# Folding w_in's last quarters as sums and differences of its halves, and reordering the row loads, in a fused FFT and expert kernel

**The chip, the cores and the metric.** One NeuronCore of one Trainium2 chip. The metric is the device time of one launch in microseconds (us), median of several executions. In the profile PE is TensorE's matmuls, PEld its weight loads, DVE VectorE, ACT ScalarE, POOL GpSimd, SP the engine that issues most of the transfers.

## The reference

```python
# x: 8 x 3008 x 256, w_in: 256 x 2048, w_out: 2048 x 256, all float32
X = np.fft.fft(np.fft.fft(x, axis=1), axis=2).real    # 2-D DFT, real part
h = X.reshape(24064, 256) @ w_in
g = h * np.cos(h)
out = g @ w_out
```

## The kernel before

The DFT over the 256 channels is never carried out on x: it is multiplied into w_in. Each quarter (512 columns) of w_in becomes cosine weights `Wc` and sine weights `Ws`; this is "a fold of a quarter". The symmetry of the DFT halves the channels: rows of x are added to and subtracted from their mirror images, which gives the E part (sums) and the O part (differences). Matmuls with the constants `MC` make from them the real and imaginary sequences `Rr` and `Ir`. Then come 376 equal steps of about 5 us. A step makes P = Wc·Rr, adds Q = Ws·Ir in the same bank, and takes h_plus = P + Q and h_minus = 2P - (P + Q); `E` is ACT's copy of 2P, so Q may only start when E is done. Sines, products g and the second matmuls X1 and X2 (with `w` and `WT`) follow. The events of the steps are sorted by a planned time; T = 4.8 us is the period of the plan, not of the chip.

The order of the first loads, and the fold of a quarter:

```python
    for j in ORDER:                       # (0, 3, 2, 1): the four row tensors of x
        load_x(0, j)                      # two plain loads each
    for g in gathers(0, ORDER):           # two indirect loads each
        gather_x(*g, table=None if g[1] else first_ix)
    CC = cpool.tile([128, 512], FP, tag="CC")
    ... # cut: definitions
    spin(out=CC, in_=CC_dr.ap())          # channel cosines and sines
    load_w1(0)
    load_mats(0)
    load_w1(1)
    ... # cut
    def fold_mms(q, part, tag):
        ps = bank(tag)
        for h in range(2):                # both halves of the 256 channels
            mm(ps, CC[:, h * 256 + part : h * 256 + part + 128], w1[q][:, h], h == 0, h == 1)
        return ps
    def fold_copy(q, ri):
        act((Ws if ri else Wc)[:, q * 512 : (q + 1) * 512], pending.pop((q, ri)))
    ... # cut
    def mm_Q(i):
        first_mm(i, Ws, Ir, 127)
```

The start of the program: dummy matmuls, then the first quarter, DVE's folds of x and the first DFTs:

```python
    def warm(n):
        w = bank("M")
        for _ in range(n):
            mm(w, ones[:, 0:128], ones[:, 128:640], True)
    warm(72)
    ... # cut
    fold_mm(0, 1)
    fold_mm(0, 0)
    ... # cut
    fold_now("e0 o0 e3 o3 e2 E2 S0 e1 R0")
    halve_now(0, VE[3])
    first_x = Dft(0, 0, 0, fold_first(), Rb, True)
    ... # cut: copies, the first matmuls of the DFTs
    fold_now("o2 O2 o1 O0 J0")
    add_O(2, 0)
    halve_now(1, VO[3])
```

In the row folds the two sources are channels 1 to 127 and their mirror images, `src[:, :, 1:128]` and `src[:, :, 255:128:-1]`, with steps 1 and -1.

## Time and profile before

| | kernel before |
|---|---|
| time, three runs | 1924.75 us (1924.59 to 1925.07) |
| the profiled run | 1924.51 us, span 1922.5 us |
| PE busy | 1905.5 us, 99% of the span |
| granted clock after 15 us | 1.00 in each stretch of 5 us |

PE is busy nearly all the time, so a change to the opening counts only by when PE enters its long row of steps. The prediction below shows PE's, DVE's and ACT's lines. Two lines of DVE's timeline (start, length, what it computes, and in brackets the idle time before), then two of the groups by shape on POOL (count, busy us, mean ns of one, idle before):

```profile
11.93 1.21 DVE L375 TENSOR_TENSOR e<-xl 96x1016 f32<-96x1016 f32 x1 [0.33 <-issue]
...
21.26 1.60 DVE L375 TENSOR_TENSOR e<-e 96x512 f32<-96x512 f32 x3
```

```profile
L375 POOL TENSOR_TENSOR o<-xl 96x635 f32<-96x635 f32 x19 | 28.4, 1493 | 0.0
L375 POOL TENSOR_TENSOR e<-xl 96x635 f32<-96x635 f32 x17 | 27.5, 1617 | 0.0
```

Before the fold of the second row tensor DVE stands for 0.33 us ("issue": the profile names no releaser), and the E part is finished at 21.26 + 1.60 = 22.86. POOL's row folds take 1.5 to 1.6 us for 635 columns.

### The profile page before, as it was taken

How to read it: one execution, taken by the hardware profiler on the slowest of the kernel's cores; microseconds unless marked ns; L12 is line 12 of the kernel's file. 1: busy time of each engine (PE TensorE's matmuls, PEld its weight loads, DVE VectorE, ACT ScalarE, POOL GpSimd, SP SyncE). 2: the span in 40 equal slices, each digit the busy share in tenths (PEclk: the TensorE clock that was granted, in tenths of full speed). 3: DMA queues.
4: the chain of work that ended last, by engine and by line, in shares of the span. 5: the costliest groups of instructions: out<-in, count | busy, mean ns of one | idle time of the engine just before them, and what ended most of it. 6: DMA issues, size and time to landing. Idle time of an engine off the chain costs nothing.

```text
span 1922.5 us, 28941 instructions
## 1 busy us (share of the span) xinstructions
PE 1905.5 (99%) x9011; PEld 1652.4 (86%) x9011; DVE 1451.9 (76%) x2364; ACT 1519.3 (79%) x2994; POOL 1522.4 (79%) x2045
## 2 busy tenths in 40 slices
PE   8999999999999999999999999999999999999998
PEld 4888888888888888888888888888888888888887
DVE  6898777777777777777777777777777777777777
ACT  4777788878878887888778887888878887877886
POOL 6789888988888888888889898888888676655564
PEclk9999999999999999999999999999999999999999
DMA  9524311322023122311222113311112110100101
GB/s 201 39 66 77 63 28 31 61 39 54 16 61 46 43 41 45 59 30 33 51 58 37 39 22 60 52 45 30 27 29 37 21 21 16 17 12 12 23 10 25
DMA packets 259969, 80.58 MB, mean 42 GB/s; under 512 B 240393, under 2 KB 243256, under 8 KB 259816
## 3 DMA queue, kind: packets, MB, share of 16 engines
q1 hardware_dynamic: 248456, 48.65, 15.1%
q0 software_dynamic: 9184, 29.83, 8.4%
q8 instruction: 72, 1.18, 0.3%
q14 instruction: 81, 0.66, 0.1%
q10 hardware_dynamic: 2176, 0.26, 0.1%
HBM read 36.72 MB, written 24.69 MB: 32 GB/s over the span
## 4 chain that ended last, share of the span: by engine, by line
PE 90%; ACT 4%; DVE 4%; issue 1%; POOL 0%; DVEq 0%; POOLq 0%
PE H L298 35%; PE pC L298 16%; PE pD L298 16%; PE pB L298 15%; PE pA L298 8%; ACT G L310 1%; PE M L298 1%; DVE G L840 1%; DVE G L304 1%; ACT E L310 1%; ACT z L310 1%; ACT M L310 1%; DVE v L304 1%; ACT H L310 0%; DVE M L304 0%
## 5 line engine op out<-in xcount | busy, mean ns | idle before, releaser
L307 POOL TENSOR_TENSOR G<-G 128x256 f32<-128x256 f32 x1500 | 1084.4, 734 | 351.4 <-DVE G L840 277.2
L840 DVE SCALAR_TENSOR_TENSOR G<-H,G 128x512 f32<-128x512 f32 x376 | 259.2, 689 | 219.0 <-ACT G L310 216.6
L304 DVE TENSOR_TENSOR G<-H,G 128x512 f32<-128x512 f32 x376 | 259.7, 691 | 214.5 <-ACT G L310 211.3
L298 PE MATMUL H<-Ir,Ws 127*128 127x256 f32 x1504 | 387.7, 379 | 4.0 <-ACT E L310 4.0
L298 PE MATMUL H<-Rr,Wc 128*128 128x256 f32 x1504 | 388.1, 380 | 0.9 <-ACT H L310 0.9
L298 PE MATMUL pC<-G,WT 128*128 128x256 f32 x1504 | 387.5, 380 | 0.7 <-DVE u L304 0.7
L310 ACT ACTIVATE H<-Rb,wex 128x256 f32<-128x256 f32 x752 | 359.9, 479 | 23.6 <-DVE G L840 9.8
L310 ACT ACTIVATE G<-H 128x512 int32<-128x512 f32 x376 | 223.8, 595 | 178.7 <-DVE G L304 177.8
L310 ACT ACTIVATE E<-H 128x512 f32<-128x512 f32 x376 | 223.8, 595 | 163.2 <-PE H L298 161.7
L298 PEld LDWEIGHTS H<-Ir,Ws 127*128 127x128 f32 x1504 | 283.5, 189 | 48.6 <-ACT E L310 8.5
L298 PEld LDWEIGHTS pC<-G,WT 128*128 128x128 f32 x1504 | 285.2, 190 | 42.7 <-PE H L298 1.5
L298 PEld LDWEIGHTS H<-Rr,Wc 128*128 128x128 f32 x1504 | 281.4, 190 | 40.8 <-ACT H L310 3.0
L310 ACT ACTIVATE G<-G,halfpi 128x512 f32<-128x512 f32 x376 | 269.3, 716 | 2.7 <-DVE G L304 1.8
L304 DVE TENSOR_TENSOR G<-E,H 128x512 f32<-128x512 f32 x376 | 255.5, 679 | 5.3 <-PE H L298 5.3
L304 DVE TENSOR_TENSOR M<-G,M 128x512 f32<-128x512 f32 x376 | 257.6, 685 | 0.0
L840 DVE SCALAR_TENSOR_TENSOR G<-G,M 128x512 f32<-128x512 f32 x376 | 254.4, 677 | 0.5 <-ACT M L310 0.5
L310 ACT ACTIVATE M<-M,halfpi 128x512 f32<-128x512 f32 x376 | 245.6, 653 | 0.0
L298 PE MATMUL pB<-G,WT 128*128 128x256 f32 x752 | 224.6, 380 | 0.2 <-POOL G L307 0.2
L298 PE MATMUL pA<-G,w 128*128 128x256 f32 x752 | 223.8, 379 | 0.0
L310 ACT ACTIVATE M<-G 128x512 int32<-128x512 f32 x376 | 223.7, 595 | 0.0
L298 PE MATMUL pB<-G,w 128*128 128x256 f32 x752 | 223.7, 379 | 0.0
L298 PE MATMUL pD<-G,WT 128*128 128x256 f32 x752 | 223.7, 379 | 0.0
(164 smaller groups left out, 2066.0 us busy)
## 6 DMA issues: line engine op xcount, KB each, us to landing
out_dram<-ot SPq DMA_DIRECT2D x496, 32.0 KB
xl<-in_x_dram SPq DMA_DIRECT2D x64, 192.0 KB
e<-e POOLq DMA_DIRECT2D x22, 384.0 KB, 4.9
o<-o POOLq DMA_DIRECT2D x22, 381.0 KB, 4.8
out_dram<-ot SPq DMA_DIRECT2D x256, 2.0 KB
Rb<-r SPq DMA_DIRECT2D x10, 376.0 KB
w<-in_moe_w_in_dram SPq DMA_DIRECT2D x4, 512.0 KB
out_dram<-ot SPq DMA_DIRECT2D x64, 28.0 KB
```

The source lines that it names most:

```text
L298: nc.tensor.matmul(out_, lhsT=lhsT, rhs=rhs, start=start, stop=stop, skip_group_check=True)
L304: pin(nc.vector.tensor_tensor(out=o, in0=a, in1=b, op=op))
L307: pin(nc.gpsimd.tensor_tensor(out=o, in0=a, in1=b, op=op))
L310: pin(nc.scalar.activation(out=o, in_=i, func=func, **kw))
L840: nc.vector.scalar_tensor_tensor(out=o, in0=h, scalar=TWO_PI, in1=c, op0=ALU.mult, op1=ALU.mult)
```

## The change

The intent is to take work off PE in the opening. With halves a and b of a quarter of w_in, an even output channel of the DFT needs only a + b and an odd one only a - b. Two of the four quarters are folded so: DVE makes the sums and differences, and PE needs one matmul per part in place of two. Even and odd outputs lie apart in `CC`, `Wc` and `Ws`, so the folds of x must give even and odd channels apart too: their sources now have steps 2 and -2. The row loads are put in the order in which they are wanted, and 8 + 1 dummies go.

```diff
-    for j in ORDER:
-        load_x(0, j)
-    for g in gathers(0, ORDER):
-        gather_x(*g, table=None if g[1] else first_ix)
+    CC = cpool.tile([128, 512], FP, tag="CC")
+    load_x(0, 0)
+    spin(out=CC, in_=CC_dr.ap())
+    for n, g in enumerate(gathers(0, ORDER)):
+        gather_x(*g, table=None if g[1] else first_ix)
+        if n == 1:
+            pin(nc.gpsimd.memset(L[3][0:1, 0:1], 0.0))
+    for j in ORDER[1:]:
+        load_x(0, j)
...  # cut
+    def fold_mm(q, part, tag="H"):
+        ps = pending[q, part] = bank(tag)
+        cc = CC.rearrange("p (h k d) -> p h k d", h=2, k=2)[:, :, part]
+        if q in diffs:
+            mm(ps, cc[:, 0], diffs[q] if part else w1[q][:, 0], True)
+            return
         for h in range(2):
+            mm(ps, cc[:, h], w1[q][:, h], h == 0, h == 1)
+    def half_sum(q, part):
+        a, b = w1[q][:, 0], w1[q][:, 1]
+        if part:
+            diffs[q] = (Rb if q % 2 else Rr)[:, RING - 512 :]
+            vtt(diffs[q], a, b, SUB)
+        else:
+            vtt(a, a, b, ADD)
...  # cut: two copies per part, each of 64 partitions
     def take_last(q):
+        copy = act if q > 1 else lambda o, i: pin(nc.gpsimd.tensor_copy(out=o, in_=i))
...  # cut
-            lo, hi = src[:, :, 1:128], src[:, :, 255:128:-1]
+            lo = src[:, :, 1:129].rearrange("p m (j r) -> p m r j", r=2)
+            hi = src[:, :, 255:127:-1].rearrange("p m (j r) -> p m r j", r=2)
...  # cut
-    warm(72)
+    warm(64)
...  # cut: the events of the first steps, moved; the halves summed:
+        (1.1, lambda: half_sum(2, 1)),
+        (1.1, lambda: half_sum(2, 0)),
-        (1.5, lambda: warm(3)),
+        (0.5, lambda: warm(2)),
-    dve_all(1, FOLD["Q1"])
+    for n, part in ((1, 1), (2, 0)):
+        on_dve(n, 0.62, lambda part=part: half_sum(3, part))
+    dve_all(2, FOLD["Q1"])
```

Both copies of one part of the second quarter (`fold_copy(1, 1)`) go to DVE, and the step-4 copies of quarters 1 and 2 (`take_last`) to POOL. Two smaller moves are not shown: the third and fourth quarters of w_in are loaded ahead of w_out, and the second step's E is planned at 0.3 in place of 0.9, ahead of the sines.

More of the change, by code (lines that the diff above doesn't have):

```diff
@@ L82, in _chan_consts @@
 def _chan_consts():
-    c = np.arange(256)
-    d = np.arange(129)
-    cos = np.cos(2.0 * np.pi * ((c[:, None] * d[None, :]) % 256) / 256) / TWO_PI
-    d = np.arange(1, 128)
-    sin = -np.sin(2.0 * np.pi * ((c[:, None] * d[None, :]) % 256) / 256) / TWO_PI
-    m = np.concatenate([cos[:, :128], sin, cos[:, 128:]], axis=1)
+    th = 2.0 * np.pi / 256
+    c = np.arange(256)[:, None]
+    even, odd = np.arange(0, 128, 2)[None], np.arange(1, 128, 2)[None]
+    m = np.concatenate(
+        [
+            -np.sin(th * (c * even[:, 1:] % 256)),
+            np.cos(th * (c * 128 % 256)),
+            np.cos(th * (c * even % 256)),
+            np.cos(th * (c * odd % 256)),
+            -np.sin(th * (c * odd % 256)),
+        ],
+        axis=1,
+    )
+    m /= TWO_PI
     return np.ascontiguousarray(
@@ L170 @@
     pin(nc.vector.memset(ones, 1.0))
-    pin(nc.gpsimd.memset(zero, 0.0))
     ix = cpool.tile([NP, 9], U32, tag="ix")
@@ L212, in load_first @@
         spin(out=L[1][0:1, 7 * ND :], in_=x[b : b + 1, 0, :])
-    for j in ORDER:
+    CC = cpool.tile([128, 512], FP, tag="CC")
[6 more added lines that the diff above has]
+    for j in ORDER[1:]:
         load_x(0, j)
-    for g in gathers(0, ORDER):
-        gather_x(*g, table=None if g[1] else first_ix)
-    CC = cpool.tile([128, 512], FP, tag="CC")
-    pin(nc.gpsimd.memset(CC[0:1, 0:1], 0.0))
+    pin(nc.gpsimd.memset(zero, 0.0))
     w1, MC = [], []
@@ L233, in load_w1 @@
         t = spool.tile([128, n], FP, tag=tag, bufs=bufs, name="w1")[:, 0:1024]
+        if not q:
+            pin(nc.gpsimd.memset(t[0:1, 0:1], 0.0))
         w1.append(t.rearrange("p (h c) -> p h c", h=2))
@@ L250, in load_w2 @@
         )
-    spin(out=CC, in_=CC_dr.ap())
     load_w1(0)
@@ L256 @@
     load_mats(1)
+    load_w1(2)
+    load_w1(3)
     load_w2(0, 4)
     load_w2(4, NF)
-    load_w1(2)
-    load_w1(3)
     load_mats(2)
@@ L273 @@
     Rr = cpool.tile([128, RING], FP, tag="Rr")
-    Ir = cpool.tile([127, RING], FP, tag="Ir")
+    Ir = cpool.tile([128, RING], FP, tag="Ir")
     Rb = cpool.tile([128, RING], FP, tag="Rb")
@@ L281 @@
     r4_dr = dpool.tile([1, NB], FP, tag="r4", name="r4")
-    WD = (128, 127)
-    E = [cpool.tile([128, NS * 128], FP, tag=f"e{j}", name=f"e{j}") for j in range(4)]
-    O = [cpool.tile([128, NS * 127 + 1], FP, tag=f"o{j}", name=f"o{j}") for j in range(4)]
-    Z = [cpool.tile([128, 4 * w + ri], FP, tag=f"z{ri}", name=f"z{ri}") for ri, w in enumerate(WD)]
-    for t in (O[1], O[2], O[3], Z[1]):
-        pin(nc.gpsimd.memset(t[0:NP, t.shape[1] - 1 :], 0.0))
+    WD = (129, 128)
+    E = [cpool.tile([128, NS * WD[0]], FP, tag=f"e{j}", name=f"e{j}") for j in range(4)]
+    O = [cpool.tile([128, NS * WD[1]], FP, tag=f"o{j}", name=f"o{j}") for j in range(4)]
+    Z = [cpool.tile([128, 4 * w], FP, tag=f"z{ri}", name=f"z{ri}") for ri, w in enumerate(WD)]
     def bank(tag):
@@ L292, in bank @@
         return ppool.tile([128, 512], FP, tag=tag, bufs=bufs, name=tag)
+    ADD, SUB = ALU.add, ALU.subtract
     ACC = ("pA", "pB", "pC", "pD")
@@ L310, in act, with fold_copy @@
         pin(nc.scalar.activation(out=o, in_=i, func=func, **kw))
-    def fold_mms(q, part, tag):
-        ps = bank(tag)
-        for h in range(2):
-            mm(
-                ps,
-                CC[:, h * 256 + part : h * 256 + part + 128],
-                w1[q][:, h],
-                h == 0,
-                h == 1,
-            )
-        return ps
-    pending = {}
-    def fold_mm(q, ri, tag="H"):
-        pending[q, ri] = fold_mms(q, 128 * ri, tag)
-    def fold_copy(q, ri):
-        act((Ws if ri else Wc)[:, q * 512 : (q + 1) * 512], pending.pop((q, ri)))
+    pending, diffs = {}, {}
+    def fold_mm(q, part, tag="H"):
[4 more added lines that the diff above has]
+            return
+        for h in range(2):
+            mm(ps, cc[:, h], w1[q][:, h], h == 0, h == 1)
[6 more added lines that the diff above has]
+            vtt(a, a, b, ADD)
+    def fold_copy(q, part, eng=None):
+        ps = pending.pop((q, part))
+        for W, h in ((Ws, part), (Wc, 1 - part)):
+            p, c = slice(64 * h, 64 * h + 64), slice(q * 512, (q + 1) * 512)
+            if eng is None:
+                act(W[p, c], ps[p])
+            else:
+                pin(eng.tensor_copy(out=W[p, c], in_=ps[p]))
     turned = {}
@@ L338, in take_last @@
         t = spool.tile([128, 512], FP, tag=("u", "p3")[q % 2], bufs=1, name="wl")
-        act(
-            t[96:128].rearrange("a (p f) -> a f p", f=4),
-            Ws[96:128, q * 512 : (q + 1) * 512].rearrange("a (f p) -> a f p", f=4),
+        copy = act if q > 1 else lambda o, i: pin(nc.gpsimd.tensor_copy(out=o, in_=i))
+        copy(
+            t[32:64].rearrange("a (p f) -> a f p", f=4),
+            Ws[32:64, q * 512 : (q + 1) * 512].rearrange("a (f p) -> a f p", f=4),
         )
@@ L347, in turn_last @@
         with nc.allow_non_contiguous_dma(reason="one row turned"):
-            pin(nc.gpsimd.dma_start(out=wex[q], in_=turned[q][127:128, :]))
+            pin(nc.gpsimd.dma_start(out=wex[q], in_=turned[q][63:64, :]))
     def sum_weights(i, k, tt=gtt):
@@ L375, in tto @@
         pin(eng.tensor_tensor(out=o, in0=a, in1=b, op=op))
-    ADD, SUB = ALU.add, ALU.subtract
     def fold_ops():
@@ L388, in fold_ops @@
                 (1, NS, lambda eng, c, j=j, s=src: pin(
-                    eng.tensor_copy(out=VE[j][:, :, 0:1], in_=s[:, :, 0:1])
+                    eng.tensor_copy(out=VE[j][:, :, 64:65], in_=s[:, :, 0:1])
                 ))
             ]
-            lo, hi = src[:, :, 1:128], src[:, :, 255:128:-1]
-            for key, o, op in ((f"e{j}", VE[j][:, :, 1:128], ADD), (f"o{j}", VO[j], SUB)):
+            lo = src[:, :, 1:129].rearrange("p m (j r) -> p m r j", r=2)
+            hi = src[:, :, 255:127:-1].rearrange("p m (j r) -> p m r j", r=2)
+            v = VE[j]
+            even = bass.AP(
+                tensor=v.tensor, offset=v.offset, ap=list(v.ap[:2]) + [[65, 2], [1, 64]]
+            )
+            odd = VO[j].rearrange("p m (r j) -> p m r j", r=2)[:, :, ::-1]
+            for key, o, op in ((f"e{j}", even, ADD), (f"o{j}", odd, SUB)):
                 if key in ("o1", "o3"):
@@ L396, in fold_ops @@
                 ops[key] = [
-                    (NS, 127, lambda eng, c, o=o, lo=lo, hi=hi, op=op: tto(
+                    (NS, 128, lambda eng, c, o=o, lo=lo, hi=hi, op=op: tto(
                         eng, o[:, c], lo[:, c], hi[:, c], op
@@ L483, in fold_first @@
         g = spool.tile([128, NS], FP, tag="xg", bufs=1, name="xg")[0:NP].unsqueeze(2)
-        gtt(a, c[0], c[1], ADD)
         gtt(g, c[2], c[3], ADD)
-        gtt(a, a, g, ADD)
+        gtt(a, c[0], g, ADD)
+        gtt(a, a, c[1], ADD)
         z = g[:, 0:4]
@@ L546, in __init__ @@
             self.n = NQ if kodd else NU
-            self.M = 127 if ri else 128
+            self.M = 128
             self.first_only = first
@@ L799, in mm_Q @@
     def mm_Q(i):
-        first_mm(i, Ws, Ir, 127)
+        first_mm(i, Ws, Ir, 128)
     def dbl(i):
@@ L1095, in add_by_dma @@
         pin(nc.gpsimd.dma_start(out=V[o][0:NP, 0:n], in_=V[a][0:NP, 0:n], accum_op=ADD))
-    add_E = lambda o, a: add_by_dma(E, o, a, NS * 128)
-    add_O = lambda o, a: add_by_dma(O, o, a, NS * 127)
+    add_E = lambda o, a: add_by_dma(E, o, a, NS * WD[0])
+    add_O = lambda o, a: add_by_dma(O, o, a, NS * WD[1])
     first_R, first_I = (
@@ L1102 @@
     )
+    fold_mm(0, 0)
     fold_mm(0, 1)
-    fold_mm(0, 0)
     mm(bank("H"), zero[:, 0:128], zero[:, 0:1].to_broadcast([1, 512]), True)
@@ L1109 @@
             act(L[1][0:1, 7 * ND :], L[0][0:1, 0:ND])
-        act(VE[j][:, :, 0:1], L[j][0:NP].rearrange("p (m d) -> p m d", d=ND)[:, :: (-1 if j in (1, 2) else 1), 0:1])
+        act(VE[j][:, :, 64:65], L[j][0:NP].rearrange("p (m d) -> p m d", d=ND)[:, :: (-1 if j in (1, 2) else 1), 0:1])
     fold_now("e0 o0 e3 o3 e2 E2 S0 e1 R0")
     halve_now(0, VE[3])
+    fold_copy(0, 0)
     first_x = Dft(0, 0, 0, fold_first(), Rb, True)
-    add_E(0, 1)
-    fold_copy(0, 1)
     take_last(0)
     turn_last(0)
-    fold_copy(0, 0)
+    add_E(0, 1)
+    first_R.first_part("pA")
+    fold_mm(1, 0)
+    first_R.copy_e()
+    first_R.part(1)
     first_x.first_part("pC")
-    first_R.first_part("pA")
+    first_R.plus_sum()
     first_x.copy_e()
-    first_R.copy_e()
+    fold_copy(0, 1)
+    fold_copy(1, 0)
+    fold_mm(1, 1, "pD")
     first_x.part(1)
     first_x.plus_sum()
-    first_R.part(1)
-    fold_mm(1, 1)
-    first_R.plus_sum()
     fold_now("o2 O2 o1 O0 J0")
@@ L1171 @@
         ):
+            if i == 1 and fn == dbl:
+                dt = 0.3
             if i == 0:
@@ L1226, in dve_all @@
         for units, size, fn in items:
-            k = max(1, 512 // size)
+            k = max(1, 520 // size)
             for i in range(0, units, k):
@@ L1238, in on_pool @@
         p = put("POOL", pool_room, cost, p)
-        at(p * T + 1.3, fn)
+        at(p * T + 1.3 if p > 1 else 2 * T + 0.35, fn)
         return p
@@ L1310 @@
     for t, fn in (
-        (0.1, lambda: fold_copy(1, 1)),
-        (0.11, lambda: take_last(1)),
-        (0.87, lambda: first_R.minus_sum()),
-        (0.87, lambda: first_x.minus_sum()),
-        (0.88, lambda: first_I.early("pB", "M")),
-        (0.12, lambda: turn_last(1)),
-        (T + 3.01, lambda: take_last(2)),
+        (-2.0, lambda: first_R.minus_sum()),
+        (-2.0, lambda: first_x.minus_sum()),
+        (-1.8, lambda: first_I.early("pB", "M")),
+        (-0.05, lambda: fold_copy(1, 1, nc.vector)),
+        (1.1, lambda: half_sum(2, 1)),
+        (1.1, lambda: half_sum(2, 0)),
+        (-7.3, lambda: take_last(1)),
+        (-1.6, lambda: turn_last(1)),
+        (2 * T - 0.9, lambda: take_last(2)),
         (2 * T + 2.3, lambda: take_last(3)),
-        (0.97, first_I.copy_e),
-        (1.5, lambda: warm(3)),
+        (-0.05, first_I.copy_e),
+        (0.5, lambda: warm(2)),
         (1.0, first_I.plus),
         (1.05, first_I.minus),
-        (-0.05, lambda: fold_mm(1, 0, "pD")),
-        (T + 0.5, lambda: fold_mm(2, 1)),
-        (0.3, lambda: fold_copy(1, 0)),
-        (T + 2.3, lambda: fold_mm(2, 0, "pD")),
-        (T + 2.5, lambda: fold_copy(2, 1)),
-        (2 * T + 0.05, lambda: fold_copy(2, 0)),
-        (2 * T + 0.5, lambda: fold_mm(3, 1, "pC")),
-        (2 * T + 2.25, lambda: fold_copy(3, 1)),
-        (3 * T + 0.5, lambda: fold_mm(3, 0)),
-        (3 * T + 1.0, lambda: fold_copy(3, 0)),
+        (T + 0.5, lambda: fold_mm(2, 0)),
+        (T + 2.3, lambda: fold_mm(2, 1, "pD")),
+        (2 * T - 1.0, lambda: fold_copy(2, 0)),
+        (2 * T + 0.05, lambda: fold_copy(2, 1)),
+        (2 * T + 0.5, lambda: fold_mm(3, 0, "pC")),
+        (2 * T + 2.25, lambda: fold_copy(3, 0)),
+        (3 * T + 0.5, lambda: fold_mm(3, 1)),
+        (3 * T + 1.0, lambda: fold_copy(3, 1)),
     ):
@@ L1442 @@
         (last - 8) * T,
-        lambda: nc.sync.dma_start(out=Rx4[127:128, 0:NB], in_=r4_dr),
+        lambda: nc.sync.dma_start(out=Rx4[63:64, 0:NB], in_=r4_dr),
     )
```

## The prediction

> **What bounds the kernel now.** I read the page's busy shares first, then PE's waits, then the opening engine by engine in the timeline.
>
> ```profile
> PE 1905.5 (99%) x9011; PEld 1652.4 (86%) x9011; DVE 1451.9 (76%) x2364; ACT 1519.3 (79%) x2994; POOL 1522.4 (79%) x2045
> ...
> PE H L298 <- ACT E L310: 4.0, 8, 1.7
> PE M L298 <- DVE halfpi L272: 2.0, 1, 2.0
> PE M L298 <- DVE Ir L304: 1.2, 1, 1.2
> PE H L298 <- issue: 1.1, 1, 1.1
> ```
>
> TensorE (PE) is busy all but 17 of 1922.5 us, and stretches of 200 us in the middle show 199.67 busy. So a change to the opening is worth what it does to the moment at which PE settles into its endless row of matmuls; everything after is then shifted whole. Some 7 to 9 us of the idle time lie behind the last matmul, 2.0 before the first one; the opening holds three waits:
>
> ```profile
> 2.01 18.61 PE L298 MATMUL M<-ones 128*128 128x512 bf16 x72 [2.01 <-DVE halfpi L272]
> 20.46 3.60 PE L298 MATMUL H<-w,CC 128*128 128x512 f32 x8
> ...
> 36.55 0.82 PE L298 MATMUL M<-ones 128*128 128x512 bf16 x3 [1.17 <-DVE Ir L304]
> ...
> 42.56 1.13 PE L298 MATMUL H<-Ir,Ws 127*128 127x256 f32 x4 [1.74 <-ACT E L310]
> ...
> 68.98 1.10 PE L298 MATMUL H<-MC,o 95*128 95x95 f32 x8 [1.13 <-issue]
> ```
>
> The first columns are start and length; the bracket is the idle time before it. The first row is dummy work that fills the time until the data is there. The reader is to see that PE waits for nothing from 2.0 to 35.4: the first real matmul is set by the number of dummies, not by a load. The last wait, called "issue", is a late DVE: the DVE clears that bank only at 68.51, behind a row of twist operations.
>
> ```profile
> 9.26 1.21 DVE L375 TENSOR_TENSOR e<-xl 96x1016 f32<-96x1016 f32 x1 [7.29 <-DMA xl<-in_x_dram,ix]
> ...
> 68.51 0.37 DVE L572 MEMSET H<- 128x378 f32 x1
> ...
> 41.92 0.58 ACT L310 ACTIVATE E<-H 128x512 f32<-128x512 f32 x1
> ...
> 43.90 1.16 ACT L310 ACTIVATE wl<-Ws 32x512 f32<-32x512 f32 x1
> ...
> 46.71 0.59 ACT L310 ACTIVATE E<-H 128x512 f32<-128x512 f32 x1
> ```
>
> These are DVE's first fold, kept waiting by the row loads, DVE's late clear, and ACT between two doublings E, each of which releases the second half (Q) of a step's first product on PE. ACT is gap-free from 40.7 to 52.
>
> [...] New in every row fold is a read with step 2, of float32. [...] The trace has step 2 only on a write: the 188-column DVE operations into Rr with step 2 take 350 ns, which is on the line of the step-1 ones (679 ns at 512 columns, about 1.04 ns a column over some 145), so no penalty. ACT's step-4 write (wl) takes 1.13 us where 512 contiguous take 0.60. [...] a step-2 read no run has shown yet. [...] (8 dummies in the first 3.0 us, 57 in a later 12.0), so the dummies taken away at the end are full-rate ones of 0.21 us.
>
> **The change part by part.** Removed from PE: 8 of 72 dummies and 1 of 3 later, 9 x 0.215 = 1.9 us. A fold of a quarter of w_in is four rows of 0.43 us, 1.72 in all; the last two quarters have two parts each, and with sums and differences each takes 0.86: 4 x 0.86 = 3.4 us. Together 5.4 us less PE time. The later matmuls with 128 rows in place of 127 cost the same.
>
> Added: four half sums on DVE, 4 x 0.7 us. Each fold copy becomes two of 64 partitions at the same 0.49 us (free size unchanged): 14 on ACT in place of 8, and 2 on DVE. Two of the four step-4 copies (1.17 us of ACT each) go to POOL. Net ACT +0.6 us, DVE +4.1 us. Row lengths of 128 and 129 in place of 127 and 128 add 1%.
>
> Row loads: now only one tensor's rows and CC stand before the first gathers, and the other row loads wait for the second gather. Before, eight loads (1.5 MB) shared the rings with them at 230 to 320 GB/s. I let the first fold start near 7.2 instead of 9.26; the later ones follow without gaps, so the E part ends near 20.9 (22.9 before), the O part near 29.2 (31.2).
>
> Now the walk along PE, with the lengths of before. The dummies end at 20.62 - 8 x 0.215 = 18.9. The first quarter of w_in was there by 20.4 behind CC's 256 KB, about 0.9 us at 280 GB/s; it is issued 0.6 us sooner without CC ahead: just in time. From 20.62 to 35.40 there was 14.8 us of matmuls; less the first P (0.86), which moves behind, 13.9: the I part ends at 32.8. The E part is wanted at 22.6, the O part at 30.4, so both are early by over 1 us. P fills PE during the 1.1 us in which DVE makes Ir; the first Q ends at 35.4, where it was 38.26. So far **2.8 us** gained.
>
> Then ACT decides. The first h_minus ends at 36.1 and ACT runs gap-free in its new order: two roundings 1.1, E 0.6, two sines 1.2, ext 1.0, two copies 1.0, wl 1.15, two roundings 1.1, two copies 1.0, E 0.5: E of the third step ends at 44.75; then sines 1.2 and copies 1.0 (46.95), wl 1.15, ext 1.0 (49.1). On PE: the second Q at 37.8 (0.75 idle; it was 42.56, since E now goes ahead of the sines), third P at 40.0 (0.5 idle), third Q at 44.75 (1.7 idle; 49.12 before), the first X2 at 46.95 because bank pC has to be copied out (1.35 idle), fourth P at 49.1 (0.4), fifth P at 54.7; it was 58.18. Gain **3.5 us**: the saved folds arrive, but ACT turns most of them into waits.
>
> Then DVE. PE would reach the matmuls of the second DFT (H<-MC,o) at 54.7 + 9.7 = 64.4. DVE's twist has slipped behind by one item, since the half sums took its first two places: from the fourth h_minus at 53.8, 10.5 us of work to the clear at about 64.6, then h_minus 0.6 and the last two twist additions 1.4: 66.7. Half of the DFT goes in the gap, the rest after it, and the next P is at 67.3 in place of 69.92. Gain **2.6 us**. From there the rows are equal; batches 2 to 8 are unchanged if the strided reads are free. 1924.75 - 2.6 = **1922.1**; I say 1922.0.
>
> **The rivals.** (a) Strided reads slow on DVE: [...] against it: the write with step 2 above. One in seven. (b) Strided reads slow on POOL: the row folds there are about 140 us; half more would break the step's budget (four sums of 0.73, up to 1.75 us of folds, in 4.77 us), and PE would lose tens of us. One in a hundred. (c) ACT and DVE catch up, and all 5.4 us of removed work plus part of the three waits (4.0 us) arrive: 1917 to 1919. Against it: ACT has no gap from 36 to 50 in my walk. One in seven. (d) The loads still bind: the first quarter or its constants land after 18.9, as the first is only just in time: 1 us of the gain is lost, no more.
>
> **Range and chances.** The size is 0.1 to 0.3%; 2% is 38 us, which only (b) could reach. Centre 1922.0; (c) sets the lower end, 1918.5, mild forms of (a) and (d) the upper, 1924.8. Faster by over 2%: 0.003; within 2%: 0.985; slower: 0.012.
>
> **What would show it.** Dummies ending near 18.9 and fold matmuls at once behind them; DVE's first fold near 7.2 and each still 1.2 us; first Q over at 35.4; PE idle of about 1.7 us before the third Q, put down to ACT E, and 1.35 before the first pC<-G,WT; the second DFT's matmuls split by a wait for DVE until about 66.7; POOL's e<-xl and o<-xl per column as before (1493 to 1617 ns for 635). Wrong [...] if ACT shows gaps between 36 and 50 while PE waits, or if PE has more than 1 us of new idle time beyond 110.

In the trace the first dummies took 3.0 / 8 = 0.375 us each, the later ones 12.0 / 57 = 0.21. Matmuls of 256 columns over 127 rows (Q) took 379 ns in the kernel before, over 128 rows (P) 380; and ACT's copies of 64x512 took 585 to 594 ns in the kernel after, those of 128x512 from 582 to 602 before.

## More of the kernel before

`PEclk` is the TensorE clock that the throttle granted, 1.00 being full speed.

All runs told of here were in the undisturbed ("fast") state.

The busy time of each engine by stretch (the length, then PE, PEld, DVE, ACT, POOL, each with its number of instructions, then PEclk, DMA share, GB/s) reads so from 25 and from 50 us, at full clock both times:

```profile
25.00:30.00 5.00, 5.00 (x31) 4.32 (x31) 4.86 (x6) 2.55 (x6) 1.47 (x2) 1.00 1.08 304
...
50.00:55.00 5.00, 5.00 (x21) 3.65 (x20) 3.52 (x5) 3.30 (x8) 3.24 (x5) 1.00 0.86 6
```

## The result, and the profile after

| | before | after |
|---|---|---|
| time, median of four runs, same chip | 1924.91 us (1924.59 to 1925.58) | 1931.84 us (1928.76 to 1934.14) |
| ratio | | 1.0035, 95% interval 1.0017 to 1.0052 |
| the profiled run | 1924.51 us | 1934.14 us, span 1932.3 us |
| PE busy | 1905.5 us | 1909.4 us |

A ratio is the mean time of one kernel's fast runs over that of the other's of the same rounds, so it is not quite the ratio of the medians. The change lost 7 us where the prediction said that it would win 2.7. The four runs after are spread over 5.4 us; the kernel before, over 1.0. The busy shares of the page say first that something odd happened: some 5.4 us of matmuls were removed, yet PE was busy for longer.

```profile
PE 1909.4 (99%) x8994; PEld 1654.7 (86%) x8994; DVE 1458.7 (75%) x2370; ACT 1521.5 (79%) x2998; POOL 1557.4 (81%) x2044
...
PEclk9899999999999999999999999999999999999999
```

Each digit of PEclk stands for 48 us; the second one is 8 where the kernel before had a 9. The stretches of 5 us show where (columns as above, PEclk third from the end):

```profile
25.00:30.00 5.00, 5.00 (x12) 3.39 (x13) 4.90 (x5) 0.49 (x1) 1.46 (x2) 0.50 1.11 390
...
50.00:55.00 5.00, 2.84 (x8) 1.90 (x9) 3.64 (x6) 4.92 (x9) 3.81 (x6) 0.70 1.76 6
...
75.00:80.00 5.00, 4.08 (x13) 3.55 (x14) 3.13 (x6) 1.91 (x5) 2.38 (x3) 0.66 0.00 0
```

From 25 to 30 us PE is counted as fully busy, with 12 matmul records in place of 31: it ran at half rate. In finer stretches PEclk is 0.50 from 24.70 to 31.52, from 52.01 to 58.83 and from 75.90 to 79.31 us. PE's timeline shows what stood before each such stretch:

```profile
18.59 3.60 PE L307 MATMUL H<-w,CC 128*128 128x512 f32 x8
...
24.80 1.14 PE L307 MATMUL pA<-MC,e 95*128 95x95 f32 x4 [2.30 <-ACT xb L319]
...
27.04 3.62 PE L307 MATMUL H<-w,CC 128*128 128x512 f32 x4
...
40.06 1.03 PE L307 MATMUL H<-Ir,Ws 128*128 128x256 f32 x4
...
51.21 1.34 PE L307 MATMUL H<-Ir,Ws 128*128 128x256 f32 x4 [1.97 <-ACT E L319]
53.50 2.07 PE L307 MATMUL pC<-G,WT 128*128 128x256 f32 x4 [0.95 <-ACT Wc L319]
...
74.19 0.66 PE L307 MATMUL H<-MC,o 95*128 95x95 f32 x4 [0.98 <-PE pD L307]
75.92 1.17 PE L307 MATMUL H<-MC,o 95*128 95x95 f32 x4 [1.07 <-DVE o L395]
76.88 1.97 PE L307 MATMUL H<-Rr,Wc 128*128 128x256 f32 x4
```

Three waits or pairs of waits: 2.30; 1.97 and 0.95; 0.98 and 1.07. Behind each of them the same matmuls take twice as long: half a fold of a quarter (four rows of the profile) 3.62 us, where it took 1.88 before; an X2 pair 2.07 in place of 1.03; a P 1.97 in place of 1.03. The kernel before has waits too, 1.17, 1.74 and 1.13, and none was followed by a slower clock. The releaser named for the first wait, ACT's xb, had ended at 24.62; the E part that this matmul reads was finished by DVE at 24.70. DVE's timeline shows why so late:

```profile
8.33 1.22 DVE L395 TENSOR_TENSOR e<-xl 96x1024 f32<-96x1024 f32 x1 [6.36 <-DMA xl<-in_x_dram,ix]
...
13.03 1.22 DVE L395 TENSOR_TENSOR e<-xl 96x1024 f32<-96x1024 f32 x1 [2.34 <-DMA xl<-in_x_dram,ix]
...
22.48 2.22 DVE L395 TENSOR_TENSOR e<-e 96x516 f32<-96x516 f32 x3
```

The first tensor comes 0.93 us sooner than before, the second 1.10 us later (13.03 against 11.93), behind a gap of 2.34 us; and the last three operations take 2.22 us in place of 1.60. The strided folds on DVE take 1.22 us, as before. Not so on POOL:

```profile
L395 POOL TENSOR_TENSOR o<-xl 96x640 f32<-96x640 f32 x19 | 35.9, 1891 | 0.0
L395 POOL TENSOR_TENSOR e<-xl 96x640 f32<-96x640 f32 x17 | 32.7, 1925 | 0.0
```

These are 27% and 19% longer than 1493 and 1617 ns, for 640 columns in place of 635. PE's total wait for POOL's products (pB<-G) rose from 0.2 to 1.0 us, that of its weight loads (PEld) from 2.8 to 7.3.

### The profile page after: what moved, and what is told of

Its sections match the earlier page's. It is cut to its first block, busy times and chain, and to the rows that moved or that the text cites. A ratio compares the mean times of both kernels' runs of the same rounds, so it can differ in the third digit from the quotient of the medians.

```text
span 1932.3 us, 28913 instructions
## 1 busy us (share of the span) xinstructions
PE 1909.4 (99%) x8994; PEld 1654.7 (86%) x8994; DVE 1458.7 (75%) x2370; ACT 1521.5 (79%) x2998; POOL 1557.4 (81%) x2044
## 4 chain that ended last, share of the span: by engine, by line
PE 84%; DVE 5%; ACT 5%; POOL 3%; issue 2%; DMA 0%; POOLq 0%; DVEq 0%; SPq 0%; ACTq 0%
PE H L307 33%; PE pC L307 15%; PE pD L307 15%; PE pB L307 14%; PE pA L307 7%; POOL G L316 2%; ACT G L319 2%; DVE G L863 1%; DVE G L313 1%; ACT E L319 1%; ACT M L319 1%; ACT z L319 1%; DVE v L313 1%; DVE M L313 1%; ACT H L319 1%
## 5 line engine op out<-in xcount | busy, mean ns | idle before, releaser
L307 PE MATMUL H<-Ir,Ws 128*128 128x256 f32 x1504 | 387.5, 380 | 5.1 <-ACT E L319 5.1
L307 PEld LDWEIGHTS H<-Ir,Ws 128*128 128x128 f32 x1504 | 284.2, 190 | 48.8 <-ACT E L319 10.4
L307 PE MATMUL pD<-G,w 128*128 128x256 f32 x752 | 224.1, 380 | 0.0
```

Source lines behind the costliest of these rows:

```text
L307: nc.tensor.matmul(out_, lhsT=lhsT, rhs=rhs, start=start, stop=stop, skip_group_check=True)
```

## The experiments

Theory: most of the loss is the clock, which falls behind the new waits; the rest is the late E part, VectorE and GpSimd. Rivals: the strided reads on POOL or the row loads cost the time by themselves, and the clock is only a companion. "Changed" below is the kernel after; the kernel before ran beside each set at 1924.3 to 1924.4 us (median). One of its 21 runs there took 1929.01 us at a mean clock of 0.996, so even that kernel loses its clock now and then.

**1. The first wait filled with the dummies that were there before, and more.**

```diff
-    warm(64)
+    warm(75)
```

> Changed kernel, with 75 dummies in place of 64 ahead of the first real matmul, nothing else. They end near 21.2 us, so the wait before the first matmul of the E part (2.30 us in the changed kernel) shrinks to about 0.1. Theory 'clock' (a wait of 2 us on TensorE makes its granted clock fall to half for some 5 us after it): the slow stretch at 25 to 31 us (clock 0.50 there, 3.4 us lost) is gone, the time falls by about 3.4 us to about 1928.5. Theory 'waits only' (the waits cost their own length, the low clock comes by chance): the E part still starts at 24.8, nothing is gained, 1931.8.

Measured: 1928.94 us (1928.15 to 1929.93), 1.0024 (1.0007 to 1.0041), 2.9 us better than the changed kernel's median; since one of its runs took 1928.76, the time alone does not show the gain. The first wait is 0.81 us and the clock is 1.00 from 25 to 35 us; the time went down though eleven dummies were added. But after waits of 1.34 and 1.15 it fell at 50 us:

```profile
48.76 1.13 PE L307 MATMUL H<-Ir,Ws 128*128 128x256 f32 x4 [1.34 <-ACT E L319]
51.04 2.07 PE L307 MATMUL pC<-G,WT 128*128 128x256 f32 x4 [1.15 <-ACT Wc L319]
```

So in this trace the clock theory holds for the first wait, and the dummies are not idle work: with 75 of them the clock stayed at 1.00 where with 64 it fell to 0.50.

**2. The old order of the row loads in the changed kernel.**

```diff
-    load_x(0, 0)
-    spin(out=CC, in_=CC_dr.ap())
-    ...  # the new order, as in the diff above
+    for j in ORDER:
+        load_x(0, j)
+    for g in gathers(0, ORDER):
+        gather_x(*g, table=None if g[1] else first_ix)
```

> Changed kernel with the row loads, the constants CC and the memsets in the order of the kernel before. Theory 'rows' (the new order of loads makes the later rows land later): VectorE's second row fold starts near 11.9 in place of 13.03, the E part is done near 23 in place of 24.7, the first wait is about 0.6 us and the clock stays at 1.00 there; the first Q is over near 36 in place of 40.9; about 1927. Rival (the folds themselves are slower, or the new order of VectorE is): the E part is still done near 24.7 and the time stays near 1931.8.

Measured: 1928.24 us (1927.64 to 1928.72), 1.0019 (1.0002 to 1.0036). The second tensor is folded at 12.65 and the E part starts on PE at 24.31, half a microsecond sooner than in the changed kernel (DVE ends it at 24.20; near 23 was expected); the first wait is split into 0.71 and 1.43 and the clock holds there. It also holds behind the pair 1.35 and 1.15 that brought it down in run 1, and falls behind 0.98 and 1.08 at 70 us, where it held in run 1. The same waits thus bring the clock down in one run and not in another. That fits the spread of the changed kernel's times: 1934.14 and 1933.89 us at a mean clock of 0.995, 1929.78 and 1928.76 at 0.998.

The kept traces show more. In all of them each stretch at half clock in the opening lasts 3.41 or 6.83 us, and the changes of the clock within a run lie whole multiples of 3.41 us apart. Cut at these points and at each 3.41 us between them, the pair of waits reads so, in run 1 and then in run 2 (columns as before):

```profile
47.65:51.06 3.41, 1.15 (x5) 0.70 (x5) 2.76 (x5) 3.36 (x7) 3.31 (x5) 1.00 1.63 6
```

```profile
44.02:47.44 3.42, 2.13 (x8) 1.03 (x6) 2.27 (x4) 3.33 (x6) 3.18 (x5) 1.00 1.95 3
47.44:50.85 3.41, 1.86 (x7) 1.35 (x8) 2.76 (x5) 3.36 (x6) 3.39 (x5) 1.00 1.41 8
```

In run 1 both waits lie in one such stretch, PE works for 1.15 of its 3.41 us, and half clock follows; in run 2 they are shared between two, with 2.13 and 1.86 us of work, and it does not. In the twelve traces without fillers over one row, PE worked for 1.60 us or less in the seven stretches of the opening behind which the clock fell (1.22, 1.45 and 1.38 in the changed kernel, 1.15 in run 1, 1.60 in run 2, 0.00 and 1.13 in run 7), and for 1.68 us (run 6) or more in every other stretch at full clock up to the last ones of the kernel. This was read from the traces afterwards; no run was made to test it.

**3 to 5. The waits filled with matmuls that add nothing.** First with products of one row of zeros, in the later waits (before the third Q, before the first X2, before the second DFT), without and with the 75 dummies; then with products over all 128 rows, of ones by zeros.

```diff
+    def fill(n):                                        # runs 3 and 4: one row
+        for _ in range(n):
+            mm(tiles[0].acc[1], zero[:, 0:128], zero[:, 0:1].to_broadcast([1, 512]), False, False)
+    at(2 * T + 1.5, lambda: fill(9))
+    at(2 * T + 2.5, lambda: fill(5))
+    at(i_step * T + 4.74, lambda: fill(9))
...
+    Zf = Rx4.bitcast(BF)                                # run 5: 128 rows, with warm(75)
-            mm(tiles[0].acc[1], zero[:, 0:128], zero[:, 0:1].to_broadcast([1, 512]), False, False)
+            mm(tiles[0].acc[1], ones[:, 0:128], Zf[:, 0:1].to_broadcast([128, 512]), False, False)
```

Run 3, one row, 64 dummies:

> Changed kernel with matmuls that add zeros into an accumulator, put into the three later waits: 9 before the third Q, 5 before the first X2, 9 before the second DFT. They take no time from the path where they are shorter than the wait. Theory 'clock': clock 1.00 from 50 to 80 us (0.70, 0.62 and 0.66 before), some 3 and 1.5 us won, about 1927.5. Theory 'waits only': 1931.8 or a little more.

Measured: 1930.93 us (1929.80 to 1935.32), 1.0039 (1.0022 to 1.0056). A miss, though PE never stopped issuing there. Two lines of its timeline and one of its stretches:

```profile
47.62 2.12 PE L307 MATMUL pB<-zero 1*128 1x512 bf16 x9
49.67 1.49 PE L307 MATMUL H<-Ir,Ws 128*128 128x256 f32 x4
51.10 2.31 PE L307 MATMUL pB<-zero 1*128 1x512 bf16 x5
53.34 2.08 PE L307 MATMUL pC<-G,WT 128*128 128x256 f32 x4
```

```profile
50.00:55.00 5.00, 5.00 (x13) 2.38 (x12) 2.79 (x5) 4.87 (x9) 3.74 (x6) 0.53 1.73 8
```

Run 4, one row, 75 dummies:

> Both fillings. Theory 'clock': granted clock 1.00 in the whole opening, all the runs alike within 1 us (the changed kernel's own runs spread over 5.4 us because some of them lose fewer stretches than others), about 1925.5. Theory 'waits only': 1931.8, and the spread stays.

Measured: 1930.86 us (1928.90 to 1933.54), 1.0038 (1.0021 to 1.0055); clock 0.66 from 50 to 55 us. A miss for the same reason. Run 5, 128 rows:

> As a_warm_fill (75 dummies first, 9 + 5 + 9 fillers in the later waits), but each filler multiplies all 128 rows of ones with zeros, where it was one row before. In a_warm_fill the clock still fell to 0.66 at 50 to 55 us though TensorE was issuing all the time. Theory 'rows count' ([...] one-row fillers are as good as a wait): clock 1.00 all through the opening, about 1.7 to 3 us less than a_warm_fill, 1927 to 1928. Theory 'fillers cost more than they save' : 1930.9 as a_warm_fill.

Measured: **1927.05 us** (1926.95 to 1927.55), 1.0014 (0.9997 to 1.0030); the four runs lie within 0.6 us, and the clock is 1.00 in each stretch of 5 us. The same place:

```profile
46.89 2.12 PE L307 MATMUL pB<-Rx,ones 128*128 128x512 bf16 x9
48.85 1.02 PE L307 MATMUL H<-Ir,Ws 128*128 128x256 f32 x4
49.72 1.25 PE L307 MATMUL pB<-Rx,ones 128*128 128x512 bf16 x5
50.80 1.02 PE L307 MATMUL pC<-G,WT 128*128 128x256 f32 x4
```

```profile
50.00:55.00 5.00, 4.81 (x21) 3.18 (x20) 3.00 (x6) 4.50 (x9) 4.77 (x7) 1.00 1.68 8
```

Runs 4 and 5 have the same dummies and fillers at the same places and differ in nothing but what a filler multiplies, and lie 3.8 us apart. So it is shown that these matmuls over one row do not reliably hold the clock (0.53 and 0.66 from 50 to 55 us in runs 3 and 4) where those over 128 rows do (1.00 in run 5), and that holding it throughout, with the dummies and fillers that this takes, is worth 1931.84 - 1927.05 = 4.8 us of the changed kernel's median. (Behind the nine one-row fillers at the DFT the clock did not fall, 1.00 from 70 to 80 us in run 3. And the weights of a filler were zeros over one row and ones over 128, so the number of rows was not parted from the values.) At full clock the changed kernel is still 2.7 us slower by the medians (1927.05 against 1924.31); the interval, which takes in the 1929.01 of the kernel before, reaches just below 1.

**6. The step-4 copies of the last two quarters moved from ACT to POOL** (with 75 dummies), to see whether ACT's row is what Q and X2 wait for.

```diff
-        copy = act if q > 1 else lambda o, i: pin(nc.gpsimd.tensor_copy(out=o, in_=i))
+        copy = lambda o, i: pin(nc.gpsimd.tensor_copy(out=o, in_=i))
```

> a_warm (75 dummies) with the turned copies of the third and fourth quarter (1.15 us each) moved from ScalarE to GpSimd, as the change did for the first two. Theory 'ScalarE is the limit between 38 and 50 us': the waits before the third Q (1.34) and before the first X2 (1.15) shrink by about 1.1 us each, time 1928.9 - 1.5 to 2 = about 1927. Rival ('GpSimd is as full, and its sums for X1 and X2 come later'): the wait only changes its name to POOL, 1928.9.

Measured: 1929.56 us (1927.03 to 1931.94), 1.0031 (1.0014 to 1.0048). The third Q's wait is gone and X2's is 0.23 us, so ACT was their cause. But PE now waits for POOL, 1.67 us at 47.77 and 0.91 at 55.04, and DVE still releases the second half of the DFT at 70.40. At full clock (the fastest of its runs, 1927.03, was the profiled one) it is no better than run 5.

**7. The half sums moved from DVE to POOL**, beside DVE's folds of the O part (with 75 dummies).

```diff
-            vtt(diffs[q], a, b, SUB)
+            gtt(diffs[q], a, b, SUB)
-            vtt(a, a, b, ADD)
+            gtt(a, a, b, ADD)
```

(The four calls were also moved ahead, to POOL's gap behind the E part.)

> a_warm (75 dummies) with the four half sums on GpSimd at 26 to 31 us, where it stands idle, instead of on VectorE, and VectorE's own fold Q1 back in its earlier places. Theory 'the half sums push VectorE's twist back': the two waits before the second DFT (0.96 and 1.07 in a_warm) fall to about 1 in sum or less, and h_minus of the first step comes earlier; about 1927. Rival ('GpSimd slows VectorE's O part[...]'): the O part is done later than 33.4 and the gain is lost, 1929.

Measured: 1935.34 us (1934.62 to 1936.23), 1.0057 (1.0040 to 1.0074), a clear miss. POOL's sums hold up DVE's folds (from 26.95 us three rows of DVE's timeline take 8.30 us, where they took 4.39 in the changed kernel), the O part comes late, and the clock is 0.66 from 35 to 45 us, behind the wait:

```profile
37.00 1.17 PE L307 MATMUL pB<-MC,o 95*128 95x95 f32 x4 [4.24 <-DVE o L395]
```

**8. The new order of the row loads alone, in the kernel before.** The edit is the reverse of run 2's.

> Kernel before with the new order of the row loads alone. Theory 'rows' (the first row tensor lands 1 to 1.5 us sooner, the other three 1 to 1.5 us later): first fold at about 8.0 (9.26), second tensor's at about 13 (11.93), E part done near 23.9 (22.9); TensorE stands at its dummies and folds until 24.3, so that nearly all is hidden: 1924.3 to 1925. Rival ('landing order helps', as the change intends): E part done before 22.9.

Measured: 1927.74 us (1924.94 to 1929.49), 1.0018 (1.0002 to 1.0035): 1924.94 and 1926.05 at a mean clock of 0.999, 1929.44 and 1929.49 at 0.996. The E part comes no sooner (finished at 23.1, before at 22.86). What comes later is a small transfer that ACT's first additions need: the first line is the kernel with the new order, the second the kernel before.

```profile
33.11 0.99 ACT L313 ACTIVATE H<-Rb,wex 128x256 f32<-128x256 f32 x2 [3.39 <-DMA wex<-wl]
```

```profile
30.95 0.99 ACT L310 ACTIVATE H<-Rb,wex 128x256 f32<-128x256 f32 x2 [1.51 <-DMA wex<-wl]
```

The first P waits 1.52 us for it. So the new order is a loss by itself, without any other part of the change, if a narrow one: 0.6 and 1.7 us above the median of the kernel before in the two runs at full clock, 5 us in the two that lost some of it. It buys the first tensor (folded 0.93 us sooner in the changed kernel) at the cost of what follows.

**9 and 10. Two repairs on top of run 5.** Run 9 issues the first half of the second DFT 2.2 us later, behind X1, with fewer fillers (5 and 4, none at the DFT); run 10 gives the first step-4 copy back to ACT, since DVE's last three operations of the E part ran beside POOL's copy.

```diff
-    i_step = plan_dft(0, 1, 1, 10, held(1, (O[2],)))
+    i_step = plan_dft(0, 1, 1, 10, held(1, (O[2],)), late=2.2)     # run 9
-        copy = act if q > 1 else ...
+        copy = act if q != 1 else ...                              # run 10
```

> a_full (75 dummies, full-array fillers, clock 1.00 throughout, 1927.05) with the first half of the second DFT moved on TensorE from ahead of the seventh step's first product to behind the X1 after it, 2.2 us later, and its 9 fillers taken out (5 and 4 fillers in the two other waits). Theory 'what is left of the loss is the wait for VectorE's twist' (the DFT's second half starts at 70.95 in a_full): the wait is gone, everything behind is about 2 us earlier, 1925. Rival ('VectorE is behind in any case'): the wait comes back at the next h_minus or X1 as VectorE or GpSimd, 1926.5 to 1927.

Measured: 1926.23 us (1926.01 to 1927.33), 1.0011 (0.9994 to 1.0028), 0.8 us better than run 5 (the later DFT and the fewer fillers were not tried apart). The wait at the DFT is gone and comes back in part, as 0.69 us for POOL at 70.46 and 0.46 for ACT at 75.11.

> a_full with the turned copy of the first quarter back on ScalarE, which stands idle there, instead of GpSimd. Theory 'contention' (GpSimd's copy at 23.3 to 24.6 us slows VectorE's two last operations of the E part, 728 ns each in the changed kernel against 420 before): they take about 425, the E part is done 0.6 us sooner, 1926.4. Rival ('rows of 129 elements are slow for VectorE'): 728 stays, 1927.05.

Measured: 1926.34 us (1926.04 to 1926.99), 1.0010 (0.9994 to 1.0027), 0.7 us better than run 5. The three operations take 1.61 us again:

```profile
22.66 1.61 DVE L395 TENSOR_TENSOR e<-e 96x516 f32<-96x516 f32 x3
```

So POOL's copy beside them had cost 0.6 us; the two short ones among them take 424 ns here and 728 in the changed kernel.

**11 and 12. All repairs together:** the old order of the row loads, 69 dummies, the first step-4 copy on ACT, the late DFT, 5 and 4 fillers over 128 rows; and, in run 12, also the fourth quarter folded by two passes as before, without its half sums.

```diff
-    for n, part in ((1, 1), (2, 0)):                               # run 12
-        on_dve(n, 0.62, lambda part=part: half_sum(3, part))
-    dve_all(2, FOLD["Q1"])
+    dve_all(1, FOLD["Q1"])
```

> Meant to beat both: the changed kernel with the old order of row loads, 69 dummies, the first turned copy on ScalarE, the later DFT and full-array fillers. By the theories 'clock', 'rows', 'contention' and 'twist' together: 1927.05 - 2 - 0.6 - 0.7 = about 1923.7, clock 1.00, runs within 1 us of each other. If one of them fails, 1925 or more.

Measured: **1924.98 us** (1924.61 to 1925.43) against 1924.39 before, 1.0004 (0.9987 to 1.0020), above the 1923.7 expected. It beats the changed kernel by 6.9 us and does not beat the one before.

> c_best with the fourth quarter folded in the old way, in two matmul passes: 1.7 us more of TensorE work, 1.4 to 1.8 us less of VectorE work. Theory 'VectorE is the limit up to 70 us': no slower than c_best, perhaps 0.5 us faster. Rival ('TensorE is the limit again once the waits are gone'): 1.7 us slower than c_best, 1925.4.

Measured: 1927.16 us (1926.68 to 1927.44), 1.0014 (0.9997 to 1.0030), 2.2 us slower than run 11. One fold of a quarter in two passes costs 1.7 us of PE, so with the other repairs in place saved matmuls do arrive: PE is the limit again. The profile also shows a wait of 0.74 us before the E part, which run 11 had not; how much of the 2.2 us is that was not separated.

**Where the time is lost, over the length of the kernel.** For each step I took the start of its P on PE in the profiled run, less the start of the same P in the kernel before:

| start in the kernel before, us | changed | run 5, full clock | run 8, old kernel, new row order | run 11, repaired |
|---|---|---|---|---|
| 109.18 | +8.17 | +1.93 | +1.69 | -0.77 |
| 166.74 | +9.60 | +3.17 | +1.63 | +0.42 |
| 509.57 | +10.51 | +4.04 | +1.61 | +1.22 |
| last matmul, 1915.02 | +10.01 | +3.36 | +1.58 | +0.54 |

Up to 109 us the columns differ by what happens in the opening: the clock is 8.17 - 1.93 = 6.2 us of it in this profiled run. Behind it, run 8 keeps its lag, and the three kernels with strided folds lose 1.2 to 1.4 us between 109 and 167 us, 0.8 to 0.9 more until 510, and get 0.5 to 0.7 back later. In run 11 PE waits there twice for POOL, 0.52 us and, at 159.12, 0.28:

```profile
148.88 0.70 PE L304 MATMUL pB<-G,WT 128*128 128x256 f32 x2 [0.52 <-POOL G L313]
```

The kernel before waits 0.17 us once. PE thus waits for POOL, whose row folds fall in the same stretch and have grown by a fifth or more. Over the whole kernel PE's weight loads wait 7.7 us for POOL's products in run 5 and 8.3 in run 11, against 2.8 before and 2.7 in run 8. No run undid the strides on POOL alone, so that they are the cause of this part is argued from the waits and from run 8 as the control, not shown (run 8 also lacks the sums and the other moves); between 167 and 510 us the loss comes in steps too small to be listed as waits, and what they are stays open.

## Why the prediction was wrong

The prediction said 1922.0 us, 1918.5 to 1924.8; the kernel took 1931.84. "Within 2%" was right, and says little where the matter is 0.1 to 0.5%.

1. **The step that failed: each wait was charged its own length.** The walk along PE was made "with the lengths of before", that is, at full clock throughout, although it forecast two waits close together, of 1.7 and 1.35 us. The waits came: second Q 0.80 us (said 0.75), third P 0.37 (0.5), third Q 1.97 (1.7), first X2 0.95 (1.35), the DFT in two halves with a wait for DVE (0.98 and 1.07). What they cost was more: the matmuls behind them ran at half rate for several us (from 24.80 to 32.06 PE did in 7.26 us what took 3.9 before). Run 5 against the result puts 4.8 us on this term, which the sum did not have. Of the 9.8 us between forecast and result, 2.1 more went with the repairs of run 11 (1927.05 to 1924.98), the load order among them; 3.0 are left, in part points 5 and 6. The prediction had seen that PE's first dummies are slower than the later ones (8 in the first 3.0 us, 57 in a later 12.0), and did not ask whether PE can become slow again.
2. **The step on the row loads: "the later ones follow without gaps".** The first fold was to be at 7.2 and came at 8.33; the second tensor then left DVE idle for 2.34 us. The E part was said to be there at 20.9 and early by over 1 us; it was finished at 24.70, and PE stood for 2.30 us. The old order was better in run 2, and the new one a loss in the old kernel in run 8. 0.6 us of the lateness is the copy moved to POOL (run 10), which the prediction had counted as relief for ACT only.
3. **The dummies as removable time: partly wrong.** They ended at 18.76 (said 18.9), and the folds followed at once. But the matmul behind the folds could not start, so the 1.7 us taken away turned into waiting, and the clock fell with it. Putting them back made the kernel faster (run 1).
4. **The saved folds: right in size.** A part takes 1.02 us in two rows where it took 1.88 in four, four times over. At full clock none of it arrived until the other engines' part was repaired (run 11), and there only -0.77 us of it at 109 us.
5. **The half sums on DVE: 0.7 us each, mis-sized.** They took 0.70, 1.10, 0.68 and 1.12 us. The long ones are the sums, written in place; POOL was at work beside all four, so what made two of them long is not shown. Mis-sized too were ACT's new copies: a pair took 1.10 to 1.23 us between 45.84 and 53.47, where the walk had 1.0. And in the walk for DVE 53.8 and 10.5 make 64.3, not 64.6, and 6.9 us, not 7 to 9, lie behind PE's last matmul; neither changes the result much.
6. **Strided reads.** On DVE they are free, 1.22 us for 1024 columns against 1.21 for 1016: rival (a) fell. On POOL they, or the shorter runs that come with them (64 columns in place of 127), cost 19 to 27% (1925 and 1891 ns for 640 columns against 1617 and 1493 for 635; which of the two it is was not measured): rival (b) was too high in its size (tens of us) and the "one in a hundred" too low for its kind. The prediction's own budget had no room for even that: four sums of 0.73 and 1.75 us of folds are 4.67 us of a step of 4.77, and a fifth more on the folds is over. The net lag behind 109 us in run 5, which is put down to this by argument, is 1.4 us (3.36 - 1.93). "PE has more than 1 us of new idle time beyond 110" was named as a sign of failure, and came: 1.31 us from 110 to 170, where the kernel before has 0.16.
7. **Rival (c), everything arrives**, was wrong, as ACT and DVE did bind. **Rival (d), the loads still bind**, was the right one in kind, held to 1 us and tied to the first quarter of w_in; it was x's second tensor.

The end position of the first Q was said to be 35.4 us; it was 40.06 + 1.03. Of that, 2.2 us came from the late E part and most of the rest, some 3.4 us as half of 24.70 to 31.52, from the half clock; from there on all predicted places were late, while the predicted waits between them stayed right.

## What to carry to other kernels

A wait on TensorE can cost more than its length (here 2.30 us of waiting were followed by 6.8 us at a clock of 0.50): before matmuls are taken away or moved, add up the idle time that will stand close together (here the clock fell behind stretches of 3.41 us in which PE worked for 1.60 us or less, and not behind those with 1.68 or more), and leave, or put in, work over all 128 rows there, beside which the clock was 1.00 in run 5; the matmuls over one row of zeros did not do (0.53 in run 3, 0.66 in run 4). When work is removed from the busiest engine, look first at what the other engines deliver at that moment, since idle time on the one that was hidden by that work becomes a wait (here 1.97 us for ACT's E before the third Q). And an earlier load is paid for by the loads behind it (here the first tensor was folded 0.93 us sooner, the second 1.10 us later): judge a new order by the last tensor that is wanted, not by the first.
